# Reading a linear-attention memory in products of 136 columns, numerators beside denominators, three products to a PSUM bank

## The chip, the cores and the metric

The kernel runs on one core of one Trainium2 chip. Times are device microseconds (us) of that core. TensorE (PE in the profile, PEld for its weight loads) multiplies into PSUM; VectorE (DVE), ScalarE (ACT) and GpSimd (POOL) work elementwise; SyncE (SP) issues most transfers. The metric is the median over the runs shown.

## What is computed

The reference mixes two branches on the same input x (2048 rows of 512, bf16) with a gate from x: `g * a + (1 - g) * b`. Branch b is a gated feed-forward block with 1792 hidden columns. Branch a is attention with 32 heads of 16 columns over four segments of 512 rows. Inside a segment it is causal softmax attention; from segment to segment a memory is carried per head. Cut to what matters for the change:

```
pq = phi(qs)                                  # phi(t) = t+1 where t>0, else exp(t)
num = einsum('bhld,bhde->bhle', pq, M)
den = einsum('bhld,bhd->bhl', pq, z)[..., None] + 1e-06
o = g * (num / den) + (1.0 - g) * a_dot       # g = sigmoid(beta), one per head
M = M + einsum('bhld,bhle->bhde', phi(ks), vs);  z = z + sum over l of phi(ks)
```

The first segment has no memory to read; the three others do.

## The kernel before, in words

**Tiling.** The 32 heads form four chunks of eight heads, 128 rows of head columns each (`NC8` = 4). Queries and keys lie transposed, 128 head columns by 512 positions (QT, ktb, pq for phi of the queries). A segment's 512 positions are four tiles of 128 (`KT` = 4). The memory M of a chunk is spread over a 128 x 128 block-diagonal matrix Mn (eight blocks of 16 x 16, made by a mask in `u_mask`, L571), z over a 128 x 8 matrix Mz (L582).

**The memory read.** In `u_den` (L595), once per pair of chunks, eight products of 8 columns (L603) put the denominators of two chunks into a PSUM tile zd; VectorE adds 1e-6 (L610), and a period later takes the reciprocal (L613) and multiplies by gh = sigmoid(beta) (L614), into rdm. In `mem_num` (L628), once per chunk, four products of 128 columns (L632) fill a PSUM tile mn, and one VectorE instruction (L636) multiplies it with rdm into tm. A DMA on SP's queue (L644) transposes tm into mT, and `add_mem` (L698) adds mT to the chunk's softmax part in oT some periods later.

**What sets the order.** The order of all instructions is written out by a planner in the kernel's Python. Its main loop (L992) runs over 72 "visits", here called periods. Each begins with a group of query-key products into the only lg tile (`group_qk`, L647), whose exponential on ScalarE (L658) gives pT, and GpSimd clears the parts above the diagonal (L662). Eight periods or so make a chunk; two periods after its last one a "lump" (L934) runs the 64 small products with V into two PSUM tiles od (`pv`, L667), which VectorE then transposes to oq, normalises (L690, L691), transposes back into oT (L696) and, from the second segment on, adds mT to (L699).

Between these the planner fills TensorE's time with units of other streams: keys kT (L375), queries qT (L289), values vT (L413) and zT (L429), the feed-forward's gate gT (L472), up uT (L493) and down dT (L509) products, and the output projection aT (L532). A unit has TensorE time, VectorE time and a due period; `fill_to` (L781) takes the one with the smallest due period, corrected by how much VectorE work is booked (`backlog`). Each unit's result is evicted from PSUM by VectorE (L312, L499, L314, L538) or, where the planner sees room, by ScalarE (`cast`, L305). Deferred work stands in `due` and is run at its period (`later`, L319).

All these PSUM tiles (kT, qT, vT, zT, gT, uT, dT, aT, od, zd, mn, MT) share one pool of four banks (L82, `pgen`); lg has the other four. A unit's first product waits until the bank that it was given has been evicted. VectorE, ScalarE and TensorE each work in their order.

Before the change, the numerator of a chunk is asked for one period ahead of the chunk's last (L1037) and runs in the middle of the next period's filling (L1031), with 0.3 us of TensorE and `EVAC` = 0.69 us of VectorE booked for it (L968); `can_num` (L974) forces the denominators where they are late.

A second path for large inputs, `general()` (L1104), is built behind a test of the inputs' size and doesn't run with these inputs.

Of the kernel before, what the change touches and what calls it, by code (L numbers as in the profile page):

```python
# [13 lines left out]
P = 128  # L14
D = 512
H = 32
# [37 lines left out]
def kernel(  # L54
# [29 lines left out]
    def const(shape, dtype, name):  # L84
        return cpool.tile(shape, dtype, name=name, tag=name)
# [10 lines left out]
    bm = const([P, 8, 17], BF, "bm")  # L96
    eo = const([P, 2], F32, "eo")
    beta = const([P, H], BF, "beta")
    gh = const([P, H], F32, "gh")
    og = const([P, H], F32, "og")  # L100
    Macc = const([P, NC8, 2, 17], F32, "Macc")
    Mn = [const([P, NC8, 128], BF, f"Mn{i}") for i in range(2)]
    Mz = [const([P, NC8, 8], BF, f"Mz{i}") for i in range(2)]
    rdm = [const([P, KT, H], F32, f"rdm{i}") for i in range(2)]
    ktb = const([P, NC8, L], BF, "ktb")
    pk = const([P, KT, D], BF, "pk")
    G = [const([P, HS, L], BF, f"G{i}") for i in range(NG)]
# [17 lines left out]
    def gen(name):  # L125
        return pgen.tile([P, 512], F32, name=name, tag="gen")
# [85 lines left out]
        nc.gpsimd.memset(Macc[:, :, :, :], 0.0)  # L212

    def setup_beta():
        eb = wk2.tile([P, H], F32, name="eb", tag="eb")
        nc.scalar.activation(eb[:, :], beta[:, :], AF.Exp, scale=-1.0)
        nc.vector.tensor_scalar_add(eb[:, :], eb[:, :], 1.0)
        nc.vector.reciprocal(gh[:, :], eb[:, :])
        nc.vector.tensor_scalar(out=og[:, :], in0=gh[:, :], scalar1=-1.0, scalar2=1.0,
                                op0=ALU.mult, op1=ALU.add)  # L220
        for j in range(4):
            r = slice(32 * j, 32 * j + 32)
            nc.vector.tensor_copy(
                ogs[r, :, :],
                og[r, :].rearrange("p (c j q) -> p c j q", c=NC8, j=4)[:, :, j, :])
# [93 lines left out]
    def later(n, f):  # L319
        due.setdefault(clock[0] + n, []).append(f)  # L320
# [5 lines left out]
    def count(key):  # L326
        return done.get(key, 0)
# [243 lines left out]
    def u_mask(s):  # L571
        def half(h0):
            for c in (h0, h0 + 1):
                nc.vector.tensor_tensor(
                    out=Mn[s % 2][:, c, :].rearrange("q (j p d) -> q j p d", j=4, p=2),
                    in0=Macc[:, c, None, :, 0:16].to_broadcast((P, 4, 2, DH)),
                    in1=bm[:, :, 0:16].rearrange("q (j p) d -> q j p d", j=4), op=ALU.mult)
            passed(0.0, 0.6)
            done["Mn", s] = count(("Mn", s)) + 1

        def f():
            nc.vector.tensor_tensor(  # L582
                out=Mz[s % 2][:, :, :].rearrange("q c (j p) -> q c j p", j=4),
                in0=Macc[:, :, None, :, 16].to_broadcast((P, NC8, 4, 2)),
                in1=bm[:, None, :, 16].to_broadcast((P, NC8, 8))
                .rearrange("q c (j p) -> q c j p", j=4), op=ALU.mult)
# [8 lines left out]
    def u_den(s, pair):  # L595
        def f():
            assert general_now[0] or ("q", s, 2 * pair) in ready
            T = gen("zd")
            Tv = T[:, 0:KT * 16].rearrange("p (q h) -> p q h", q=KT)
            for cc in range(2):  # L600
                c = 2 * pair + cc
                for qq in range(KT):
                    nc.tensor.matmul(Tv[:, qq, 8 * cc:8 * cc + 8],  # L603
                                     lhsT=pq[:, c, qq * P:(qq + 1) * P],
                                     rhs=Mz[s % 2][:, c, :], start=True, stop=True)
                if cc == 0:
                    yield 0.12
            h0 = 16 * pair
            r = rdm[s % 2][:, :, h0:h0 + 16]
            nc.vector.tensor_scalar_add(r, Tv, 1e-6)  # L610

            def f_inv():
                nc.vector.reciprocal(r, r)  # L613
                nc.vector.tensor_tensor(out=r, in0=r,  # L614
                                        in1=gh[:, None, h0:h0 + 16].to_broadcast((P, KT, 16)),
                                        op=ALU.mult)
                passed(0.0, 0.8)
                done["inv", s] = count(("inv", s)) + 1
            if general_now[0]:
                f_inv()  # L620
            else:
                later(1, f_inv)
            return 0.12
        return 0.24, 0.22, f

    tms = {}

    def mem_num(s, c):  # L628
        assert general_now[0] or (count(("Mn", s)) > c // 2 and count(("inv", s)) > c // 2)
        T = gen("mn")  # L630
        for qq in range(KT):
            nc.tensor.matmul(T[:, qq * P:(qq + 1) * P],  # L632
                             lhsT=pq[:, c, qq * P:(qq + 1) * P], rhs=Mn[s % 2][:, c, :],
                             start=True, stop=True)
        tm = wk2.tile([P, KT, 8, DH], BF, name="tm", tag="tm")
        nc.vector.tensor_tensor(  # L636
            out=tm[:, :, :, :], in0=T[:, :].rearrange("p (q h d) -> p q h d", q=KT, h=8),
            in1=rdm[s % 2][:, :, 8 * c:8 * c + 8, None].to_broadcast((P, KT, 8, DH)), op=ALU.mult)
        mT = wk2.tile([P, L], BF, name="mT", tag="mT")
        mTv = mT[:, :].rearrange("p (q t) -> p q t", q=KT)  # L640
        if general_now[0]:
            turn(mTv, tm[:, :, :, :].rearrange("p q h d -> p q (h d)"))
        else:
            nc.sync.dma_start_transpose(mTv, tm[:, :, :, :].rearrange("p q h d -> p (q h d)"))  # L644
        tms[(s, c)] = mT

    def group_qk(pieces):  # L647
        lg = plg.tile([P, 4, 512], F32, name="lg", tag="lg")
# [78 lines left out]
    def passed(pe, dve=0.0):  # L727
        backlog[0] = max(0.0, backlog[0] - pe) + dve
        t_pe[0] += pe
# [155 lines left out]
    us = []  # L885
    for s in range(NSEG - 1):
        us.append(unit(u_mask(s + 1), 0, None, lambda s=s: count(("M", s)) == 1))
        us += [unit(u_den(s + 1, pair), NP * s + 16 + 9 * pair, ("den", s + 1),
                    lambda s=s, pair=pair: ("q", s + 1, 2 * pair) in ready)
               for pair in range(2)]  # L890
    streams.append(Stream("M", us))

    us = [unit(u_absmax_x(2, (18, 20, 22, 25)), 17, None, lambda: clock[0] >= 17),
# [71 lines left out]
        if s > 0:  # L965
            later(4, f_add)

    def numerator(s, c):  # L968
        room_for_bank()
        mem_num(s, c)  # L970
        done["num", s] = count(("num", s)) + 1
        passed(0.3, EVAC)

    def can_num(s, c):  # L974
        if count(("den", s)) <= c // 2 and ("q", s, c - c % 2) in ready:
            need(("den", s), c // 2 + 1)
        return count(("Mn", s)) > c // 2 and count(("inv", s)) > c // 2

    asked = []
    pending = []  # L980
    visits = []
    for i in range(0, NSEG * NC8, 2):
# [9 lines left out]
    for pieces in visits:  # L992
# [41 lines left out]
        fill_to(goal)  # L1034
        t_pe[0] = max(t_pe[0], ready_at)
        limit[0] = 0.0
        for i in range(NC8, NSEG * NC8):  # L1037
            if last(i) - 1 == clock[0]:
                asked.append((i // NC8, i % NC8))
        if asked and can_num(*asked[0]):  # L1040
            pending.append(lambda a=asked.pop(0): numerator(*a))
    limit[0] = 1e9
    fill_to(t_pe[0] + TAIL_FILL * 0.42)
    assert not asked
    for f in pending:
        f()
    for _, i in lumps:
# [56 lines left out]
    def general():  # L1104
# [4 lines left out]
        for s in range(NSEG):  # L1109
# [16 lines left out]
            if s > 0:  # L1126
                for c in range(0, NC8, 2):
                    phi_now(pq[:, c:c + 2, :], QT[:, c:c + 2, :])
                run(u_mask(s))
                run(u_den(s, 0))  # L1130
                run(u_den(s, 1))
            neg = G[(s + 1) % NG][:, 8, 0:P]
            nc.gpsimd.memset(neg, 0.0)
            nc.gpsimd.affine_select(out=neg, in_=neg, pattern=[[-1, P]], compare_op=ALU.is_ge,
                                    fill=-1e9 * DH ** 0.5, base=0, channel_multiplier=1)
            for c in range(NC8):
                o2 = wk2.tile([P, 16, 2, DH], BF, name="o2", tag="o2")
                if s > 0:
                    mem_num(s, c)
                tiles = {}  # L1140
                for b in range(5):
                    t = ptp.tile([P, 4, 512], BF, name="pT", tag="pT")
                    tiles[b] = (t, 0)
                    if 1 <= b <= 3:
                        tiles[NB - b] = (t, L - 64 * b)
                general_blocks(s, c, tiles)
                oq = pv(s, c, tiles)
                for p in range(2):
                    norm(c, p, oq[p], o2)
                back(c, o2, oT)  # L1150
                if s > 0:
                    add_mem(s, c, oT)
# [54 lines left out]
```

## Time and profile before

| | us |
|---|---|
| median of 3 runs (268.22 to 268.45) | 268.25 |
| the profiled execution | 268.14 |
| its span, first to last instruction | 266.3 |
| VectorE's busy time in 28 to 250 us (222 us) | 171.2 |
| TensorE's busy time in 28 to 250 us | 221.95 |
| granted TensorE clock | 1.0 |

The groups of the memory read, with number, busy time and mean of one:

| line | engine | what | number | busy us | mean ns |
|---|---|---|---|---|---|
| L603 | PE | zd, 128 x 8 | 48 | 2.1 | 166 |
| L632 | PE | mn, 128 x 128 | 48 | 4.6 | 219 |
| L610 | DVE | sum with 1e-6, 128 x 64 from PSUM | 6 | 1.3 | 216 |
| L613 | DVE | reciprocal, 128 x 64 | 6 | 3.2 | 526 |
| L614 | DVE | times gh, 128 x 64 | 6 | 1.8 | 308 |
| L636 | DVE | tm, 128 x 512 from PSUM | 12 | 8.2 | 682 |
| L644 | SP | DMA transpose of tm | 12 | | 2.4 us to landing |

A product's row lasts until its result has drained, so products overlap: what one costs TensorE is the distance from its start to the next start. Likewise two VectorE instructions that don't depend on each other overlap a little at their ends.

### The profile page before, as it was taken

The numbers are of one execution on the slowest core, as the hardware profiler recorded it, in microseconds if no ns is written. First come the engines' busy times: TensorE is split into PE (matmuls) and PEld (weight loads), VectorE is DVE, ScalarE is ACT, GpSimd is POOL, SyncE is SP. The second block draws the span as 40 slices with busy tenths as digits, with TensorE's granted clock in tenths as the row PEclk, the third lists the DMA queues.
The fourth block names the chain that finished last, engine by engine and source line by source line (L and its number), as shares of the span: only waits on it lengthen the run. The fifth ranks groups of instructions, "written<-read, shape, count | busy, mean of one in ns | idle before, by whom it ended". The sixth has DMA issues, their size and how long they took to land.

```text
span 266.3 us, 6883 instructions
## 1 busy us (share of the span) xinstructions
PE 261.7 (98%) x2865; PEld 117.4 (44%) x2865; DVE 200.7 (75%) x394; ACT 209.7 (79%) x164; POOL 155.0 (58%) x298
## 2 busy tenths in 40 slices
PE   7999999999999999999999999999999999999995
PEld 4454434344443444444445344444444444444443
DVE  2999574969569887698887858695978759698364
ACT  4236889988998899889999999889989987657511
POOL 3000158896716979678940899687694099654500
PEclk9999999999999999999999999999999999999999
DMA  7999931200322001300023010301000110002202
GB/s 217 328 194 290 323 78 39 42 4 1 68 57 42 2 0 42 79 6 20 2 59 86 0 23 20 64 20 22 20 23 23 46 22 8 14 20 42 41 22 84
DMA packets 30410, 16.60 MB, mean 62 GB/s; under 512 B 20008, under 2 KB 29096, under 8 KB 30376
## 3 DMA queue, kind: packets, MB, share of 16 engines
q1 hardware_dynamic: 30232, 16.07, 24.2%
q8 instruction: 23, 0.38, 0.6%
q14 instruction: 11, 0.09, 0.1%
q10 hardware_dynamic: 144, 0.07, 0.1%
HBM read 8.14 MB, written 2.10 MB: 38 GB/s over the span
## 4 chain that ended last, share of the span: by engine, by line
PE 98%; DVE 1%; issue 0%; DVEq 0%
PE uT L493 19%; PE dT L509 19%; PE gT L472 19%; PE lg L653 9%; PE od L678 7%; PE kT L375 5%; PE qT L289 5%; PE aT L532 5%; PE vT L413 5%; PE mn L632 1%; PE warm L166 1%; PE zT L429 1%; PE MT L560 1%; DVE tB L538 1%; PE x0T L183 1%; PE zd L603 0%
## 5 line engine op out<-in xcount | busy, mean ns | idle before, releaser
L662 POOL TENSOR_SCALAR_AFFINE_SELECT pT<-pT 64x256 bf16<-64x256 bf16 x256 | 112.2, 438 | 94.6 <-ACT pT L658 81.8
L658 ACT ACTIVATE pT<-lg 128x2048 bf16<-128x2048 f32 x72 | 135.1, 1876 | 22.5 <-PE lg L653 21.2
L493 PE MATMUL uT<-x,wup 128*128 128x512 bf16 x224 | 60.6, 380 | 0.0
L472 PE MATMUL gT<-x,wga 128*128 128x512 bf16 x224 | 55.6, 379 | 0.0
L509 PE MATMUL dT<-wdn,G 128*128 128x512 bf16 x224 | 53.9, 380 | 0.0
L499 DVE TENSOR_TENSOR G<-uT,G 128x512 bf16<-128x512 f32 x56 | 38.1, 683 | 6.2 <-PE uT L493 5.7
L385 POOL TENSOR_SCALAR KTm<-ktb,eo 128x512 bf16<-128x512 bf16 x26 | 40.6, 1575 | 1.3
L685 DVE STREAM_TRANSPOSE oq<-od 128x512 f32<-128x512 f32 x32 | 21.0, 696 | 19.9 <-PE od L678 19.9
L472 PEld LDWEIGHTS <-wga 128*128 128x128 bf16 x224 | 20.7, 98 | 24.5 <-issue 2.4
L509 PEld LDWEIGHTS <-G 128*128 128x128 bf16 x224 | 20.5, 98 | 24.3 <-issue 2.8
L493 PEld LDWEIGHTS <-wup 128*128 128x128 bf16 x224 | 20.2, 98 | 24.5 <-issue 4.7
L653 PE MATMUL lg<-QT,KTm 32*128 32x192 bf16 (+7 forms) x512 | 28.6, 287 | 0.0
L312 DVE CAST G<-gT 128x512 bf16<-128x512 f32 x25 | 17.2, 686 | 5.8 <-PE gT L472 5.6
L653 PEld LDWEIGHTS <-KTm 32*128 32x128 bf16 x512 | 8.5, 92 | 29.5 <-issue 29.5
L678 PE MATMUL od<-pT,V 64*32 64x128 bf16 (+7 forms) x512 | 19.3, 284 | 0.0
L678 PE MATMUL od<-pT,Vs 64*32 64x128 bf16 (+7 forms) x512 | 18.9, 284 | 0.0
L487 ACT ACTIVATE G<-G 128x3584 bf16<-128x3584 bf16 x6 | 18.8, 3182 | 0.0
L691 DVE SCALAR_TENSOR_TENSOR o<-oq,ogs,rden 128x256 bf16<-128x256 f32 x32 | 17.3, 541 | 1.1
L375 PE MATMUL kT<-x,wk 128*128 128x512 bf16 x64 | 16.6, 379 | 0.4 <-DVE eo L204 0.4
L289 PE MATMUL qT<-x,wq 128*128 128x512 bf16 x64 | 16.6, 379 | 0.0
L538 DVE SCALAR_TENSOR_TENSOR tB<-aT,gct,tB 128x512 bf16<-128x512 f32 (+1 forms) x18 | 12.0, 685 | 5.7 <-PE aT L532 5.5
L532 PE MATMUL aT<-wo,oT 128*128 128x512 bf16 (+1 forms) x72 | 16.2, 356 | 0.0
(95 smaller groups left out, 269.7 us busy)
## 6 DMA issues: line engine op xcount, KB each, us to landing
wup<-in_B_w_up_dram SPq DMA_DIRECT2D x1, 1792.0 KB, 9.7
wdn<-in_B_w_down_dram SPq DMA_DIRECT2D x1, 1792.0 KB
out_dram<-tB SPq DMA_DIRECT2D x13, 128.0 KB, 1.7
wga<-in_B_w_gate_dram SPq DMA_DIRECT2D x1, 1280.0 KB, 10.4
Vs<-V SPq DMA_DIRECT2D x8, 144.0 KB, 3.1
G<-in_A_x_dram SPq DMA_DIRECT2D x2, 256.0 KB, 2.8
wk<-in_A_wk_dram SPq DMA_DIRECT2D x2, 256.0 KB, 4.5
wq<-in_A_wq_dram SPq DMA_DIRECT2D x1, 512.0 KB, 5.6
```

What stands on the lines that cost most here:

```text
L289: nc.tensor.matmul(T[:, :], lhsT=wq[:, fc, c * P:(c + 1) * P], rhs=xS[s % NX][:, fc, :], start=(fc == 0), stop=(fc == FC - 1))
L375: nc.tensor.matmul(T[:, :], lhsT=wk[:, fc, c * P:(c + 1) * P], rhs=xS[s % NX][:, fc, :], start=(fc == 0), stop=(fc == FC - 1))
L385: eng.tensor_scalar(out=KTm[:, (NC8 * s + c) % NK, :, p, :], in0=ktb[:, c, :].rearrange("q (b k) -> q b k", b=NB), scalar1=eo[:, p:p + 1], ...
L472: nc.tensor.matmul(T[:, :], lhsT=wga[:, fc, hs * P:(hs + 1) * P], rhs=xS[s % NX][:, fc, :], start=(fc == 0), stop=(fc == FC - 1))
L493: nc.tensor.matmul(T[:, :], lhsT=wup[:, fc, hs * P:(hs + 1) * P], rhs=xS[s % NX][:, fc, :], start=(fc == 0), stop=(fc == FC - 1))
L499: nc.vector.tensor_tensor(out=g, in0=T[:, :], in1=g, op=ALU.mult)
L509: nc.tensor.matmul(T[:, :], lhsT=G[s % NG][:, hs, qt * P:(qt + 1) * P], rhs=wdn[:, hs, :], start=(hs == 0), stop=(hs == HS - 1))
L532: nc.tensor.matmul(T[:, 0:w], lhsT=oT[:, fc, qt * P:(qt + 1) * P], rhs=wo[:, fc, d0:d0 + w], start=(fc == 0), stop=(fc == FC - 1))
L653: nc.tensor.matmul(lg[:, j, off:off + n], lhsT=KTm[rows, i % NK, b].rearrange("r p k -> r (p k)"), rhs=QT[rows, i % NC8, 64 * b:L], start= ...
L658: nc.scalar.activation(pT[:, :, :], lg[:, :, :], AF.Exp, scale=DH ** -0.5)
L662: nc.gpsimd.affine_select(out=v, in_=v, pattern=[[0, 4], [1, 64]], compare_op=ALU.is_ge, fill=0.0, base=0, channel_multiplier=-1)
L678: nc.tensor.matmul(od[p][32 * j:32 * j + 32, 64 * b:L], lhsT=w[:, 18 * h:18 * h + 32], rhs=t[rows, j, off:off + n], start=(b == 0), stop=( ...
```

## The change

Mz and rdm go; Mn becomes 136 columns wide, 128 numerator columns and 8 denominator columns, so one product gives both for one tile of positions. `u_den` and `mem_num` are replaced by `mem_read`. The 16 products of a segment (four chunks by four tiles) are read three to a bank, in six reads (products 0-2, 3-5, 6-8, 9-11, 12-14 and 15); where a read holds products of two chunks, its VectorE work is done in two parts, except the reciprocal. The denominators are multiplied by eb = 1 + exp(-beta) in the same instruction that adds 1e-6, so that the reciprocal is already the factor for the numerator. The planner books 0.18 us of TensorE and 1.1 us of VectorE for a read and asks for the six reads at periods counted from the chunks' last ones.

```diff
-    Mn = [const([P, NC8, 128], BF, f"Mn{i}") for i in range(2)]
-    Mz = [const([P, NC8, 8], BF, f"Mz{i}") for i in range(2)]
-    rdm = [const([P, KT, H], F32, f"rdm{i}") for i in range(2)]
+    Mn = [const([P, NC8, 136], BF, f"Mn{i}") for i in range(2)]
...
+    def mem_read(s, m):
+        T = gen("mn")
+        todo = [divmod(t, KT) for t in range(3 * m, min(3 * m + 3, NC8 * KT))]
+        rd = wk2.tile([P, 3, 8], F32, name="rd", tag="rd")
+        parts = []
+        for i, (c, qq) in enumerate(todo):
...
+            nc.tensor.matmul(T[:, 136 * i:136 * i + 136], lhsT=pq[:, c, qq * P:(qq + 1) * P],
+                             rhs=Mn[s % 2][:, c, :], start=True, stop=True)
+            if parts and parts[-1][0] == c:
+                parts[-1][3] += 1
+            else:
+                parts.append([c, qq, i, 1])
+        Tv = T[:, 0:408].rearrange("p (k e) -> p k e", k=3)
+        for c, qq, i, n in parts:
+            nc.vector.scalar_tensor_tensor(
+                out=rd[:, i:i + n, :], in0=Tv[:, i:i + n, 128:136], scalar=1e-6,
+                in1=eb[:, None, 8 * c:8 * c + 8].to_broadcast((P, n, 8)),
+                op0=ALU.add, op1=ALU.mult)
+        nc.vector.reciprocal(rd[:, 0:len(todo), :], rd[:, 0:len(todo), :])
+        for c, qq, i, n in parts:
+            if qq == 0:
+                halves[s, c] = wk2.tile([P, KT, 8, DH], BF, name="tm", tag="tm")
+            tm = halves[s, c]
+            nc.vector.tensor_tensor(
+                out=tm[:, qq:qq + n, :, :],
+                in0=Tv[:, i:i + n, 0:128].rearrange("p q (h d) -> p q h d", h=8),
+                in1=rd[:, i:i + n, :, None].to_broadcast((P, n, 8, DH)), op=ALU.mult)
+            if qq + n < KT:
+                continue
...
+                nc.sync.dma_start_transpose(mTv, tm[:, :, :, :].rearrange("p q h d -> p (q h d)"))
+            tms[(s, c)] = mT
+            done["num", s] = count(("num", s)) + 1
...
-        us += [unit(u_den(s + 1, pair), NP * s + 16 + 9 * pair, ("den", s + 1),
-                    lambda s=s, pair=pair: ("q", s + 1, 2 * pair) in ready)
-               for pair in range(2)]
...
-    def numerator(s, c):
+    def read(s, m):
         room_for_bank()
-        mem_num(s, c)
-        done["num", s] = count(("num", s)) + 1
-        passed(0.3, EVAC)
+        mem_read(s, m)
+        passed(0.18, 1.1)
...
+    reads = [(last(NC8 * s + c) - back_, s, m) for s in range(1, NSEG)
+             for c, back_, m in ((0, 2, 0), (0, 1, 1), (1, 1, 2), (2, 1, 3), (3, 2, 4), (3, 1, 5))]
...
-        for i in range(NC8, NSEG * NC8):
-            if last(i) - 1 == clock[0]:
-                asked.append((i // NC8, i % NC8))
-        if asked and can_num(*asked[0]):
-            pending.append(lambda a=asked.pop(0): numerator(*a))
+        if reads and reads[0][0] <= clock[0] and can_read(*reads[0][1:]):
+            pending.append(lambda a=reads.pop(0)[1:]: read(*a))
```

More of the change, by code (lines that the diff above doesn't have):

```diff
@@ L98 @@
     beta = const([P, H], BF, "beta")
-    gh = const([P, H], F32, "gh")
+    eb = const([P, H], F32, "eb")
     og = const([P, H], F32, "og")
     Macc = const([P, NC8, 2, 17], F32, "Macc")
-    Mn = [const([P, NC8, 128], BF, f"Mn{i}") for i in range(2)]
-    Mz = [const([P, NC8, 8], BF, f"Mz{i}") for i in range(2)]
-    rdm = [const([P, KT, H], F32, f"rdm{i}") for i in range(2)]
+    Mn = [const([P, NC8, 136], BF, f"Mn{i}") for i in range(2)]
     ktb = const([P, NC8, L], BF, "ktb")
@@ L214, in setup_beta @@
     def setup_beta():
-        eb = wk2.tile([P, H], F32, name="eb", tag="eb")
+        gh = wk2.tile([P, H], F32, name="gh", tag="gh")
         nc.scalar.activation(eb[:, :], beta[:, :], AF.Exp, scale=-1.0)
@@ L574, in half @@
                 nc.vector.tensor_tensor(
-                    out=Mn[s % 2][:, c, :].rearrange("q (j p d) -> q j p d", j=4, p=2),
+                    out=Mn[s % 2][:, c, 0:128].rearrange("q (j p d) -> q j p d", j=4, p=2),
                     in0=Macc[:, c, None, :, 0:16].to_broadcast((P, 4, 2, DH)),
@@ L582, in f @@
             nc.vector.tensor_tensor(
-                out=Mz[s % 2][:, :, :].rearrange("q c (j p) -> q c j p", j=4),
+                out=Mn[s % 2][:, :, 128:136].rearrange("q c (j p) -> q c j p", j=4),
                 in0=Macc[:, :, None, :, 16].to_broadcast((P, NC8, 4, 2)),
@@ L593, in u_mask @@
         return 0.0, 0.2, f
[L595 to L618, printed above, removed]
+    tms = {}
@@ new lines @@
+    halves = {}
+    def mem_read(s, m):
[4 more added lines that the diff above has]
+        for i, (c, qq) in enumerate(todo):
+            assert general_now[0] or (count(("Mn", s)) > c // 2 and ("q", s, c - c % 2) in ready)
+            nc.tensor.matmul(T[:, 136 * i:136 * i + 136], lhsT=pq[:, c, qq * P:(qq + 1) * P],
[21 more added lines that the diff above has]
+                continue
+            mT = wk2.tile([P, L], BF, name="mT", tag="mT")
+            mTv = mT[:, :].rearrange("p (q t) -> p q t", q=KT)
@@ L619, in f @@
             if general_now[0]:
-                f_inv()
+                turn(mTv, tm[:, :, :, :].rearrange("p q h d -> p q (h d)"))
             else:
[L622 to L645, printed above, removed]
@@ L966, in lump, with can_read @@
             later(4, f_add)
-    def numerator(s, c):
+    def read(s, m):
         room_for_bank()
-        mem_num(s, c)
-        done["num", s] = count(("num", s)) + 1
-        passed(0.3, EVAC)
[L974 to L979, printed above, removed]
+        mem_read(s, m)
+        passed(0.18, 1.1)
+    def can_read(s, m):
+        cs = {t // KT for t in range(3 * m, min(3 * m + 3, NC8 * KT))}
+        return all(count(("Mn", s)) > c // 2 and ("q", s, c - c % 2) in ready for c in cs)
+    reads = [(last(NC8 * s + c) - back_, s, m) for s in range(1, NSEG)
+             for c, back_, m in ((0, 2, 0), (0, 1, 1), (1, 1, 2), (2, 1, 3), (3, 2, 4), (3, 1, 5))]
     pending = []
@@ L1036 @@
         limit[0] = 0.0
-        for i in range(NC8, NSEG * NC8):
-            if last(i) - 1 == clock[0]:
-                asked.append((i // NC8, i % NC8))
-        if asked and can_num(*asked[0]):
-            pending.append(lambda a=asked.pop(0): numerator(*a))
+        if reads and reads[0][0] <= clock[0] and can_read(*reads[0][1:]):
+            pending.append(lambda a=reads.pop(0)[1:]: read(*a))
     limit[0] = 1e9
     fill_to(t_pe[0] + TAIL_FILL * 0.42)
-    assert not asked
+    assert not reads
     for f in pending:
@@ L1129, in general @@
                 run(u_mask(s))
-                run(u_den(s, 0))
-                run(u_den(s, 1))
             neg = G[(s + 1) % NG][:, 8, 0:P]
@@ L1137, in general @@
                 o2 = wk2.tile([P, 16, 2, DH], BF, name="o2", tag="o2")
-                if s > 0:
-                    mem_num(s, c)
+                for m in ((0, 1), (2,), (3,), (4, 5))[c] if s > 0 else ():
+                    mem_read(s, m)
                 tiles = {}
```

## The prediction

> **What bounds the kernel now.** I read the busy table first, then the chain that ended last, then the groups by line with shapes kept apart, then the instructions in order of time around the memory read.
>
> ```profile
> span 266.3 us, 6883 instructions
> PE 261.7 (98%) x2865; PEld 117.4 (44%) x2865; DVE 200.7 (75%) x394; ACT 209.7 (79%) x164; POOL 155.0 (58%) x298
> PE 98%; DVE 1%; issue 0%; DVEq 0%
> ```
>
> TensorE is the path: its products stand one behind the other from start to end, and the chain runs along it for 98% of the span. So a product that goes saves its own share of TensorE's time, and nothing else is worth anything unless it makes TensorE wait. The second question is whether it ever waits now. In order of time (start, length, instruction) two places show what the removed and the widened products cost, and a third shows a wait:
>
> ```profile
> 73.29 0.34 PE L603 MATMUL zd<-Mz,pq 128*128 128x8 bf16 x8
> 97.53 0.39 PE L632 MATMUL mn<-Mn,pq 128*128 128x128 bf16 x4
> ...
> 136.31 0.40 PE L653 MATMUL lg<-QT,KTm 32*128 32x448 bf16 x8
> 136.64 0.39 PE L678 MATMUL od<-pT,V 64*32 64x512 bf16 x1
> 137.06 0.39 PE L678 MATMUL od<-pT,Vs 64*32 64x512 bf16 x1
> ```
>
> The two od products of 136.64 and 137.06 belong to the two banks of one chunk and elsewhere start 3 ns apart; here the second waits 0.42 us for its bank. VectorE, in the same stretch, is why:
>
> ```profile
> 133.30 0.68 DVE L636 TENSOR_TENSOR tm<-mn,rdm 128x512 bf16<-128x512 f32 x1
> 133.89 0.69 DVE L574 TENSOR_TENSOR Mn<-Macc,bm 128x128 bf16<-128x128 f32 x2
> 134.51 0.70 DVE L696 STREAM_TRANSPOSE oT<-o 128x512 bf16<-128x512 bf16 x1
> 135.13 0.55 DVE L346 TENSOR_SCALAR ktb<-ktb 128x1024 bf16<-128x1024 bf16 x1
> 135.72 0.69 DVE L351 TENSOR_TENSOR ktb<-phe,ktb 128x1024 bf16<-128x1024 bf16 x1
> 136.32 0.68 DVE L499 TENSOR_TENSOR G<-uT,G 128x512 bf16<-128x512 f32 x1
> ```
>
> VectorE runs from 127.41 (the oq transposes of the chunk before) to 137.00 without a gap, 9.59 us; the product uT at its end frees the bank at 137.00. So the cover is thin: VectorE is idle a quarter of the span, but not here. A like wait of 0.25 us stands at 227.0, where GpSimd's selects are late. I found no other.
>
> **Part 1, TensorE.** Eight products of 8 columns take 0.34 us with 166 ns for one alone: (340 - 166)/7 = 25 ns from start to start. 48 go: -1.2 us. Four of 128 columns: (390 - 219)/3 = 57 ns; those of 256 columns (the last aT) stand 109 ns apart, so 136 columns cost 8/128 of 53 = 3.3 ns more: 48 x 3.3 = +0.16 us. In the changed order the weights are loaded 48 times fewer; loads already lie beside products. Changes between full-array and split-array products, at about 95 ns each, are 166 in both orders. Sum: **-1.04 us**. Bounds: nothing gained at the widest (136 columns at the 109 ns of 256 would be +2.5, which the even steps between the rows exclude), -1.2 if the 8 columns are free.
>
> **Part 2, VectorE's work.** In a crowded stretch an instruction starts before the last has ended: the 512-column evictions stand 0.60 apart (133.30 to 133.89) with 0.68 each, 0.08 less than the row; one that needs its predecessor's result starts 0.035 after it. Removed per pair of chunks: sum 0.13 (0.215 less 0.08), reciprocal 0.56, product 0.14, so 6 x 0.83 = 5.0 us; and 12 tm of 0.60, 7.2 us. Added, 18 reads. None of the new shapes is in the trace, so by neighbours: the add-and-scale from the bank between 0.15 (4 columns from a bank, L442) and 0.28 (128 columns, L437), I take 0.21, that of L610; the reciprocal of 24 between 0.24 (16) and 0.35 (32), I take 0.29; tm of 384, 256, 128 columns between 0.28 (L437) and 0.68, on the line between them 0.55, 0.41, 0.28. A read of one part: 0.245 + 0.33 + 0.47 = 1.04 us; of two parts 1.24; the last (one product) 0.68. Per segment 3 x 1.04 + 2 x 1.24 + 0.68 = 6.3, in all 18.9. Net **+6.7 us of VectorE** (from 4 to 9 by the ends), with one cast more on it. Beside TensorE's work, this is nothing where VectorE has slack; the planner books 1.1 for a read, so it does not overlook it. Masks, beta's setup (gh and eb change places) and the 12 transposing DMAs keep their number; those land in 2.4 us and are needed some four periods later, and SP's queue passes them over one or two output writes. The general path does not run.
>
> **Part 3, where the slack is missing.** A read now holds its bank through three to five VectorE instructions. The first waits for the last product of the three; behind it on VectorE stand the evictions of gT, uT and aT, and for their banks waits TensorE. The changed kernel was built, not run, so its order is known. I summed rows per period (a period is one trip of the loop at L992 and begins with its lg products; 72 in all) along that order, VectorE against TensorE, and followed the bank of each tile where VectorE is behind.
>
> Periods 34 to 38 (the stretch above). The changed order has in VectorE's run the reads of products 12 to 14 and of product 15, instead of one tm, and od's second bank is freed by the eviction of aT, which stands behind the two ktb instructions. So the run is 9.59 - 0.60 + 1.04 + 0.68 + 0.66 = 11.4 us from the oq transposes, which start 1.28 after the first od. TensorE's work from that od to the next: 34 products at 0.216, four of 0.06, four lg at 0.425, od 1.2: 10.5 us. Wait 1.28 + 11.4 + 0.06 - 10.5 = 2.2 us, against 0.42 now: **+1.8** (1.2 to 2.3 by the ends of part 2).
>
> Periods 39 to 41. Reads 0 and 1 of the next segment stand in neighbouring periods with the gates. From period 39's start the eviction of its uT ends at 0.33 (lg) + 8 x 0.216 + 0.2 to arrive + 0.6 = 2.87; then 0.68 (norm), 0.75 (gates, 83.08 to 83.83), gT 0.60, read 1.04, uT 0.60, oT 0.63, pq 0.55, gT 0.60: 8.3. The down product that takes this last bank is due at 7.6 (periods 39 and 40 with 10 and 9 products, 2.6 and 2.55, and 2.45 of period 41): **+0.75** (0 to 1.1). Before, nothing waits here.
>
> At 227.0 seven dT products now stand ahead of od: its wait of 0.25 goes, **-0.25** (-0.25 to 0). Elsewhere the same sums leave 0.1 to 0.5 us to spare.
>
> Sum: -1.04 + 1.8 + 0.75 - 0.25 = +1.3. The profiled execution took 268.14 (span 266.3), 0.1 under the median of 268.25. 268.14 + 1.3 = **269.4 us**, its own range 268.8 to 270.2.
>
> [...] VectorE runs 394 instructions now and 431 in the changed order. Its dependent instructions show a gap of 35 ns, its independent ones none. [...]
>
> **Rivals.**
> - The reads stay covered, and TensorE's saving is all: 268.1 - 1.0 - 0.25 + some tenths = 267.2. For it: in 222 us VectorE is idle for 50, and four banks let it lag (around 80 to 88 it runs 8 us in one piece and no product waits). It holds if the two reads of periods 35 and 36 together stay under 0.9 us and the later one falls behind an idle moment. Against: the bounds above put them at no less than 1.2. Chance 0.17.
> - One of the two places waits, the other not: 268.3 (267.7 to 268.8). Chance 0.17.
> - VectorE becomes the pace more widely, one mechanism: TensorE takes the next bank before a read has left it. All 6.7 exposed would give 274; a third of it beyond my two places gives 271.5. Against: 98% of TensorE and the spare tenths. It decides from 0.2 us more per read. Chance 0.12 for over 270.2.
> - That the change does not do what it says is excluded by the order: no product of 8 columns is left, 48 of 136 stand there.
>
> **The numbers.** Forecast 0.54, covered 0.17, one place 0.17, wider 0.12. About 0.2% is what a measurement of this kernel can tell from no change: 267.7 to 268.8. Faster 0.18, within 0.17, slower 0.65. The range leaves out most of the covered case and the far end of the wide one: 267.5 to 271.0.
>
> **What would show it.** Right: no zd, read products 59 ns apart, VectorE at about 207 us (78%); in the period list a second od product over a microsecond behind the first near 138, and a gap before a dT near 148. Wrong: those products 3 ns apart and the span shorter by about 1.0 (then the reads are shorter than their neighbours or VectorE's run starts earlier); or a new wait of GpSimd or ScalarE, which I hold at nothing since their instructions keep their number to within three casts.

## The result, and the profile after

| | before | after |
|---|---|---|
| median, us | 268.22 (22 runs, 268.05 to 270.14) | 269.39 (22 runs, 268.48 to 271.84) |
| ratio to before | | 1.004, 95% interval 1.0025 to 1.0055 |
| the profiled execution | 268.14 | 269.79 |
| its span | 266.3 | 267.9 |
| first lg product to last product | 234.83 | 235.92 |

The change makes the kernel 0.4% slower. The last row leaves out the first 28 us, in which executions differ whatever the kernel (last section). In that stretch the profiled executions differ by 1.09 us. One execution of a kernel further below (e8) ran in a slower state of the chip, at 299.63 us and a granted clock of 0.85, and is left out of its figures.

The lines of the page after that answer to those shown of before:

```profile
span 267.9 us, 6815 instructions
PE 261.5 (98%) x2817; PEld 116.2 (43%) x2817; DVE 204.1 (76%) x431; ACT 208.9 (78%) x163; POOL 156.4 (58%) x298
PE 91%; DVE 6%; issue 1%; DVEq 0%
```

TensorE has 48 products less and is as busy as before (261.5 us against 261.7): a product's row reaches past the next one's start (for 512 columns rows of 380 ns, starts 216 ns apart), so the busy time hardly shows what a product costs. The third line tells more: the chain that ended last ran along TensorE for 98% and now for 91%; 6% has gone to VectorE, so TensorE now waits for VectorE on its way. The waits themselves are far shorter than 6% of the span, as the next lists show.

The new groups, with shapes kept apart:

```profile
L604 PE MATMUL mn<-Mn,pq 128*128 128x136 bf16 x48 | 5.8, 223 | 0.0
L612 DVE SCALAR_TENSOR_TENSOR rd<-mn,eb 128x24 f32<-128x24 f32 x9 | 1.5, 169 | 1.1 <-PE mn L604 1.1
L616 DVE RECIPROCAL rd<-rd 128x24 f32<-128x24 f32 x15 | 4.5, 303 | 0.5
L621 DVE TENSOR_TENSOR tm<-mn,rd 128x384 bf16<-128x384 f32 x9 | 5.0, 557 | 0.3
```

The 18 reads have 19.2 us of VectorE rows; what they replace had 14.5 (1.3 + 3.2 + 1.8 + 8.2). And the waits, in order of time, around the end of the first segment that reads a memory:

```profile
133.32 0.23 PE L604 MATMUL mn<-Mn,pq 128*128 128x136 bf16 x1
133.90 1.02 PE L287 MATMUL qT<-x,wq 128*128 128x512 bf16 x4 [0.36 <-DVE G L497]
135.19 0.38 PE L530 MATMUL aT<-wo,oT 128*128 128x512 bf16 x1 [0.26 <-DVE G L310]
...
138.41 0.39 PE L667 MATMUL od<-pT,V 64*32 64x512 bf16 x1
139.14 0.39 PE L667 MATMUL od<-pT,Vs 64*32 64x512 bf16 x1 [0.34 <-DVE tB L536]
```

Brackets show idle time ahead of a row, after the end of the row before; what a wait costs is its start-to-start distance less the usual one. That gives 0.53 before qT (0.587 less 0.059), 0.42 before aT (0.636 less 0.216) and 0.72 at od (0.724 against 0.003). VectorE's order of time in that stretch names the late work:

```profile
135.65 0.16 DVE L612 SCALAR_TENSOR_TENSOR rd<-mn,eb 128x8 f32<-128x8 f32 x1
135.84 0.20 DVE L616 RECIPROCAL rd<-rd 128x8 f32<-128x8 f32 x1
136.07 0.29 DVE L621 TENSOR_TENSOR tm<-mn,rd 128x128 bf16<-128x128 f32 x1
136.28 0.48 DVE L572 TENSOR_TENSOR Mn<-Macc,bm 128x128 bf16<-128x128 f32 x2
...
137.73 0.69 DVE L349 TENSOR_TENSOR ktb<-phe,ktb 128x1024 bf16<-128x1024 bf16 x1
138.34 0.74 DVE L536 SCALAR_TENSOR_TENSOR tB<-aT,gct,tB 128x512 bf16<-128x512 f32 x1
```

The eviction of aT into tB, which frees od's second bank, ends at 139.08, behind the last read, Mn, oT and two ktb instructions. A wait of 0.44 stands before a dT (0.651 less 0.216):

```profile
156.53 0.81 PE L470 MATMUL gT<-x,wga 128*128 128x512 bf16 x3
157.61 0.59 PE L507 MATMUL dT<-wdn,G 128*128 128x512 bf16 x2 [0.27 <-DVE G L310]
```

One stop had no place in the prediction. The 64 products of MT (the sums for the new memory, L558), which before ran in one piece of 0.67 us, break off after the 60th, for 0.70 us, and the profile names no releaser:

```profile
174.58 0.63 PE L558 MATMUL MT<-V,pk 128*32 128x34 bf16 x60
175.74 0.20 PE L558 MATMUL MT<-V,pk 128*32 128x34 bf16 x4 [0.53 <-issue]
```

I call it the hole. The od of 244.3 waits 0.12 in all (1.226 against 1.106 us for its 64 products), and the wait of 0.25 at 227.0 is gone.

### The profile page after: what moved, and what is told of

It reads as the page before. It is cut to its first block, busy times and chain, and to the rows that moved or that the text cites. A ratio compares the mean times of both kernels' runs of the same rounds, so it can differ in the third digit from the quotient of the medians.

```text
span 267.9 us, 6815 instructions
## 1 busy us (share of the span) xinstructions
PE 261.5 (98%) x2817; PEld 116.2 (43%) x2817; DVE 204.1 (76%) x431; ACT 208.9 (78%) x163; POOL 156.4 (58%) x298
## 4 chain that ended last, share of the span: by engine, by line
PE 91%; DVE 6%; issue 1%; DVEq 0%
PE dT L507 18%; PE uT L491 18%; PE gT L470 17%; PE lg L642 8%; PE od L667 7%; PE kT L373 5%; PE qT L287 5%; PE vT L411 5%; PE aT L530 5%; DVE G L497 1%; PE warm L164 1%; DVE G L310 1%; PE mn L604 1%; DVE tB L536 1%; PE MT L558 1%
## 5 line engine op out<-in xcount | busy, mean ns | idle before, releaser
L470 PE MATMUL gT<-x,wga 128*128 128x512 bf16 x224 | 57.0, 380 | 0.0
L507 PE MATMUL dT<-wdn,G 128*128 128x512 bf16 x224 | 53.1, 380 | 0.3 <-DVE G L310 0.3
L383 POOL TENSOR_SCALAR KTm<-ktb,eo 128x512 bf16<-128x512 bf16 x26 | 41.4, 1603 | 1.3
L310 DVE CAST G<-gT 128x512 bf16<-128x512 f32 x28 | 19.2, 685 | 5.7 <-PE gT L470 5.1
L530 PE MATMUL aT<-wo,oT 128*128 128x512 bf16 (+1 forms) x72 | 17.2, 357 | 0.3 <-DVE G L310 0.3
L667 PEld LDWEIGHTS <-V 64*32 64x32 bf16 x512 | 13.1, 92 | 6.0 <-issue 2.8
```

The lines of the kernel that those rows point to most:

```text
L383: eng.tensor_scalar(out=KTm[:, (NC8 * s + c) % NK, :, p, :], in0=ktb[:, c, :].rearrange("q (b k) -> q b k", b=NB), scalar1=eo[:, p:p + 1], ...
L470: nc.tensor.matmul(T[:, :], lhsT=wga[:, fc, hs * P:(hs + 1) * P], rhs=xS[s % NX][:, fc, :], start=(fc == 0), stop=(fc == FC - 1))
L507: nc.tensor.matmul(T[:, :], lhsT=G[s % NG][:, hs, qt * P:(qt + 1) * P], rhs=wdn[:, hs, :], start=(hs == 0), stop=(hs == HS - 1))
L530: nc.tensor.matmul(T[:, 0:w], lhsT=oT[:, fc, qt * P:(qt + 1) * P], rhs=wo[:, fc, d0:d0 + w], start=(fc == 0), stop=(fc == FC - 1))
L667: nc.tensor.matmul(od[p][32 * j:32 * j + 32, 64 * b:L], lhsT=w[:, 18 * h:18 * h + 32], rhs=t[rows, j, off:off + n], start=(b == 0), stop=( ...
```

## The experiments

**The theory** from the two traces: TensorE's saving is real, and three things eat it: VectorE late in two places (its extra work, and where the reads stand), and the hole, which is TensorE waiting for its own instructions. **The rivals**: the reads' VectorE work is the price everywhere; the order of the reads alone is the price; the hole belongs to the changed order.

One table carries them all. The ratios are to runs of before on the same chip, whose medians were 268.17 (beside e1 to e4), 268.46 (e5 to e8) and 268.19 (e9 to e12); they are estimated from all these runs, and so are not quite the quotients of the medians. "Stretch" is from the first lg product to the start of the last product in the profiled execution. "Place 1" sums the waits from mn to od near 133 to 139, "place 2" is the one ahead of dT (or the unit in its stead) near 157, "others" are the waits at other od groups, units and lg groups (the table leaves out what is under 0.06; the 0.08 of e12 under "hole" stands at 115 us and is told of below).

| kernel | median | ratio, 95% interval | stretch | place 1 | place 2 | hole | others | stretch less waits |
|---|---|---|---|---|---|---|---|---|
| before | 268.22 | | 234.83 | 0.42 | 0 | 0 | 0.40 | 234.01 |
| after | 269.39 | 1.004, 1.0025 to 1.0055 | 235.92 | 1.67 | 0.44 | 0.70 | 0.12 | 232.99 |
| e1_bare_all | 267.93 | 0.9994, 0.9982 to 1.0005 | 234.39 | 1.00 | 0 | 0.38 | 0 | 233.01 |
| e2_bare_p1 | 268.58 | 1.0017, 1.0008 to 1.0026 | 234.82 | 1.00 | 0.52 | 0.18 | 0.12 | 233.00 |
| e3_bare_p2 | 269.20 | 1.0039, 1.0026 to 1.0052 | 235.93 | 1.67 | 0 | 1.02 | 0.24 | 233.00 |
| e4_zd_twice | 269.65 | 1.0057, 1.0044 to 1.007 | 236.03 | 0.43 | 0 | 0 | 0.40 | 235.20 |
| e5_after_no_small_warm | 270.24 | 1.004, 1.0014 to 1.0066 | 235.26 | 1.67 | 0.44 | 0 | 0.13 | 233.02 |
| e6_before_no_small_warm | 268.42 | 1.002, 0.9997 to 1.0043 | 234.88 | 0.44 | 0 | 0 | 0.44 | 234.00 |
| e7_fold | 268.69 | 1.0011, 0.9999 to 1.0022 | 235.22 | 1.49 | 0.51 | 0.21 | 0 | 233.01 |
| e8_early | 269.40 | 1.0045, 1.0028 to 1.0061 | 236.10 | 0.23 | 0 | 0.59 | 2.21 | 233.07 |
| e9_after_more_warm | 268.75 | 1.0033, 1.0016 to 1.0051 | 235.23 | 1.67 | 0.44 | 0 | 0.12 | 233.00 |
| e12_before_more_warm | 268.32 | 1.0007, 0.9988 to 1.0026 | 234.91 | 0.42 | 0 | 0.08 | 0.40 | 234.01 |
| e11_early1_more_warm | 267.50 | 0.9985, 0.9965 to 1.0005 | 233.96 | 0.23 | 0 | 0 | 0.71 | 233.02 |
| e10_fold_early1_more_warm | 266.49 | 0.9941, 0.992 to 0.9961 | 233.06 | 0 | 0 | 0 | 0 | 233.06 |

The last column is the reading to learn from. For every kernel with products of 136 columns, whatever its waits, it comes out at 233.0 to 233.1; for before, e6 and e12, with their separate products of 8 and 128 columns, at 234.0. So no wait by which these kernels differ is left out, and TensorE's own saving is 1.01 us (234.01 less 233.00). A wait that all of them share would stay in the column unseen.

Of the "others" of before, 0.15 are two waits for ScalarE that hardly show as idle time, since the row of the product ahead lasts 380 ns: the lg groups of 109.30 and 122.77 start 51 and 52 ns after ScalarE's exponential has read the lg tile, 385 ns after the product ahead of them where 312 is usual. In order of time, before:

```profile
120.84 1.88 ACT L658 ACTIVATE pT<-lg 128x2048 bf16<-128x2048 f32 x1 [0.31 <-PE lg L653]
...
121.95 0.81 PE L493 MATMUL uT<-x,wup 128*128 128x512 bf16 x3
...
122.77 0.40 PE L653 MATMUL lg<-QT,KTm 32*128 32x512 bf16 x4
```

The exponential ends at 122.72; the last of the three uT products starts at 122.38. Before, e4, e6 and e12 have both waits; after and the kernels made from it have neither.

### Reads without their denominators

```diff
+        bare = not general_now[0]        # e2: and s == 1 and m >= 4; e3: and s == 2 and m == 0
+        if not bare:
             for c, qq, i, n in parts:
                 nc.vector.scalar_tensor_tensor(...)
             nc.vector.reciprocal(rd[:, 0:len(todo), :], rd[:, 0:len(todo), :])
...
-                in1=rd[:, i:i + n, :, None].to_broadcast((P, n, 8, DH)), op=ALU.mult)
+                in1=(eb[:, None, 8 * c:8 * c + 8, None] if bare else rd[:, i:i + n, :, None])
+                .to_broadcast((P, n, 8, DH)), op=ALU.mult)
```

> The changed kernel, its order of instructions kept, with the sum-and-scale and the reciprocal of every read left out (the numerators are multiplied by 1+exp(-beta) instead, so the memory part of the output is not the reference's). VectorE loses about 10 us of work, the products stay as they are. Theory (TensorE waits for banks behind the longer reads): the waits of periods 36 to 41 go, TensorE's saving of 1.0 is left, 267.2 to 267.6. Rival (the new order of the other units costs the time, not the reads' length): 269.4, waits where they were.

> As the run before, but the two instructions are left out in two reads alone, products 12 to 14 and 15 of segment 1 (the memory part of these is not the reference's). VectorE loses 0.53 + 0.42 = 0.95 us in its run of periods 34 to 38, where TensorE waited 1.67 us. Theory: 0.95 less, 268.4 to 268.6. Rival: 269.4.

> As the run before, but the two instructions are left out in one read alone, products 0 to 2 of segment 2 (the memory part of these is not the reference's). VectorE loses 0.53 us ahead of the eviction that the down product of 156.96 waited 0.44 us for. Theory: that wait goes, 0.4 us less, 269.0. Rival: 269.4.

e1 keeps the order of after, and VectorE has some 9 us of rows less. Its time came out 0.3 above the expected range: place 2 is gone, but place 1 keeps 1.00 of its 1.67, and the hole stays. e2 takes the two instructions away at the end of the first segment alone: place 1 goes to 1.00 as in e1, place 2 stays. e3 takes them away in one read of the next segment: place 2 goes, place 1 stays. So each place has its own cause in the reads that stand there, and what the other reads' denominators cost is at most the 0.12 under others. In place 1 the add, scale and reciprocal are worth 0.67; the other 0.6 over before remains with the reads bare. e3's time hardly moved, and can't tell the two expectations apart: its hole was 1.02 in the profiled execution. The hole has another size in each profiled execution.

### What a product of 8 columns costs

```diff
-                for qq in range(KT):
+                for qq in sorted(2 * list(range(KT))):
                     nc.tensor.matmul(Tv[:, qq, 8 * cc:8 * cc + 8],
```

> The kernel before with each of the 48 products of 8 columns done twice. Theory (25 ns from start to start on a TensorE that never rests): +1.2 us, 269.4. Rival (they lie free beside weight loads and waits): 268.2. [...]

In order of time, e4 (before with each of these products twice):

```profile
73.64 0.55 PE L603 MATMUL zd<-Mz,pq 128*128 128x8 bf16 x16
```

(0.55 - 0.166)/15 = 25.6 ns from start to start, and the stretch less waits grows by 1.19 us, 24.8 ns for each of 48. The 25 ns of the prediction hold. The median went up by 1.48 (interval of the ratio: 1.2 to 1.9 us).

### The hole, and where it stands in the instruction stream

The trace of after holds 23 transfers of 16 KB in a queue that the page calls "q8 instruction". 5634 products and weight loads by 23 are some 245 each; from one transfer's start to the next TensorE starts 254 of its instructions on average, if the last transfer, which starts after the last product, is left out. So TensorE's instructions come in blocks of about that number. Each hole comes after one of the transfers:

| kernel | transfer starts, us | takes | landed | TensorE goes on | after landing | hole |
|---|---|---|---|---|---|---|
| after | 172.80 | 1.35 | 174.15 | 175.74 | 1.6 | 0.70 |
| e1_bare_all | 171.88 | 0.88 | 172.76 | 174.36 | 1.6 | 0.38 |
| e2_bare_p1 | 172.47 | 0.98 | 173.45 | 174.90 | 1.45 | 0.18 |
| e3_bare_p2 | 172.37 | 1.40 | 173.77 | 175.17 | 1.4 | 1.02 |
| e7_fold | 172.17 | 1.10 | 173.27 | 174.73 | 1.45 | 0.21 |
| e8_early | 171.38 | 1.13 | 172.50 | 174.08 | 1.6 | 0.59 |

Whatever the transfer's start and length, TensorE goes on 1.4 to 1.6 us after it has landed. In that stretch the 64 od products end and the 64 MT products follow within 3 us, which fits a block that is used up before the next is there. In e7, which has one product less ahead of its MT group, the hole stands after the 61st product, not the 60th: in all six kernels 1885 products stand ahead of the hole. It keeps its place in the instruction stream, not in the work. To move the stream alone I changed the warming products at the very start:

```diff
-        for i in range(5):       # e9, e12 (e5, e6: unchanged)
+        for i in range(4):
...
-        for i in range(16):      # e5, e6: this loop left out
+        for i in range(48):      # with 64 columns each in place of 256
```

> After, with the 16 small products that only warm TensorE up at the very start left out (no output depends on them). Nothing later is moved; only every later product stands 16 products (32 of TensorE's instructions) earlier in its instruction stream, so that the refills of its instructions fall elsewhere. Theory (the hole of 0.2 to 1.0 us between the 60th and 61st product of the third MT group, seen in after and in the three bare kernels, is TensorE waiting for its next instructions, because the od and MT products behind that refill use them up in under 3 us): the hole is gone, the waits at mn, qT, od and dT stay as in after, 268.4 to 269.1. Rival (the hole belongs to the changed order, or to a bank or the memory sums): the hole stays at the same product, 269.2 to 269.6. Either way up to 0.5 us may go at the start itself, so the hole decides and not the time alone.

> Before, with the same 16 warming products left out. Its od and MT groups near 170 us then stand within 5 instructions of where after has them. Theory (instruction refill): a hole of 0.2 to 1.0 us comes into the last ten products of the third MT group, which had none in before; 267.9 to 269.0, with a start up to 0.5 us earlier against it. Rival (the hole belongs to the change): no hole, 267.7 to 268.2.

> After, with 48 small warming products of 64 columns in place of 16 of 256, and four large ones in place of five, so that about as long a start puts 31 products more (62 instructions) ahead of everything else. Theory (instruction refill): some 24 slow products now stand between the refill's boundary and the od products near 172 us, the block of 256 instructions lasts over 4 us instead of 2.9, and the hole in the third MT group is gone, as it was without the small products; the waits at mn, qT, od and dT stay; 268.5 to 269.0, and from the first query-key product to the end 0.2 to 1.0 us less than in after. Rival (dropping the small products took the hole away in some other way than by the count of instructions): the hole is back, 269.2 to 269.6.

> Before, with the same 48 small and four large warming products: the control for the start. Both theories: no hole in either, 268.0 to 268.5; what it differs from before by is the price of the other start, to be taken off the kernels beside it.

The third MT group of e9, in order of time:

```profile
173.97 0.40 PE L642 MATMUL lg<-QT,KTm 32*128 32x384 bf16 x8
174.30 0.67 PE L558 MATMUL MT<-V,pk 128*32 128x34 bf16 x64
```

The hole is gone with 31 products more ahead, as it was in e5 with 16 less, and the waits at places 1 and 2 are the same to 0.01 us. Median against its control e12: 268.75 - 268.32 = +0.43, where after and before lie 1.17 apart. That fits a hole worth some 0.7 us in the medians too, but the interval of each of the two ratios is 0.8 to 1.0 us wide, so the medians alone don't show it.

e6 failed to do what I expected: before, with its od and MT groups where after has them in the stream, showed no hole in its profiled execution. There the transfer started at 170.36, took 1.05 and landed at 171.41; the block ended at 172.97, 1.55 us later, within the 1.4 to 1.6 us of the table. The block lasted 3.03 us in e6, and 2.85 in after without its hole. That fits the theory, but it is a near miss, not the hole that I had asked for: that the same edit makes one in before isn't shown.

e12, the control, shows a small one where I had expected none. Its stream has before's order, 31 products later:

```profile
114.14 0.93 PE L413 MATMUL vT<-wv,x 128*128 128x448 bf16 x4
115.00 0.20 PEld L653 LDWEIGHTS <-KTm 32*128 32x128 bf16 x8 [0.37 <-issue]
115.09 0.40 PE L653 MATMUL lg<-QT,KTm 32*128 32x384 bf16 x8
```

From the last vT product to the lg product are 366 ns, where 282 are usual, 0.08 us more; ScalarE had read the lg tile 0.99 us before. A transfer landed at 113.72, 1.28 us ahead of the weight load. 2496 of TensorE's instructions stand ahead of that load in the trace, 3777 or 3778 ahead of the first instruction behind the hole in the six kernels: 1281 or 1282 apart. In after the transfer ahead of the hole (172.80) is the fifth behind the one of 114.50, which is the nearest to e12's stop; so five blocks make 1281 or 1282 instructions, some 256 each. So this stop too stands at the end of a block, and in before's order. At 0.08 us in one execution it is a small sign, but it speaks against the rival that the hole belongs to the changed order.

The profiled execution of e5 (270.39, by its median of 270.24) lost its time at the start (last section): its stretch is 0.66 shorter than that of after.

### Cheaper reads, and reads elsewhere

e7 folds 1 + exp(-beta) into the mask of the denominator columns, so that a read is two VectorE instructions:

```diff
-                in1=bm[:, None, :, 16].to_broadcast((P, NC8, 8))
-                .rearrange("q c (j p) -> q c j p", j=4), op=ALU.mult)
+                in1=bz[:, :, :].rearrange("q c (j p) -> q c j p", j=4), op=ALU.mult)  # bm's column x eb
...
+        nc.vector.reciprocal(rd[:, 0:n, :], Tv[:, :, 128:136])
+        nc.vector.tensor_tensor(out=tm[:, 3 * m:3 * m + n, :, :],
+            in0=Tv[:, :, 0:128].rearrange("p q (h d) -> p q h d", h=8),
+            in1=rd[:, 0:n, :, None].to_broadcast((P, n, 8, DH)), op=ALU.mult)
...
-        passed(0.18, 1.1)
+        passed(0.18, 0.85)
```

> After, with 1+exp(-beta) folded into the mask that makes the denominator columns, so that a read is one reciprocal from PSUM and one multiplication into one tm for all 16 products of the segment; 0.85 us booked instead of 1.1. It leaves out the sum of 1e-6 in the denominators. Reads then take about 0.86 us of VectorE (reciprocal 0.30, tm 0.56), 14.3 us in all against 19.1 in after. Theory (VectorE's lateness in two crowded places is the price): mn to qT, od at 138 and gT to dT lose half or more of what they have over the bare reads; the hole in the MT products stays; 268.2 to 268.9. Rival (the order and the six bank turns are the price, not VectorE's work): 269.2 to 269.5, the waits as in after.

e8 moves the last two reads of a segment; e11 and e10 move them in the first of these segments alone, and e10 has the fold as well:

```diff
-             for c, back_, m in (..., (2, 1, 3), (3, 2, 4), (3, 1, 5))]
+             for c, back_, m in (..., (2, 1, 3), (3, 4, 4), (3, 3, 5))]    # e8
+             for c, back_, m in (..., (2, 1, 3), (3, 4 if s == 1 else 2, 4), (3, 3 if s == 1 else 1, 5))]    # e11, e10
```

> After, with the last two reads of each segment asked for two periods earlier (four and three before the chunk's last instead of two and one), away from the new Mn, the oT and the ktb of the segment's end. Theory (price of a crowded place): the wait of 0.5 between mn and qT near 133 and most of the od wait at 138 go, VectorE has a hole before 139, 268.4 to 269.0. Rival (VectorE has nothing to spare anywhere near, the lateness only moves): waits of the same sum two periods earlier, 269.2 to 269.6.

> After with the other start, and with the last two reads two periods earlier in the first segment with a memory alone. Theory (place 1 is a matter of where two reads stand): mn to qT and qT to aT near 134 go, od at 138 keeps some 0.2, the rest stays as in after (gT to dT 0.4); 267.6 to 268.3, below the control. Rival (the lateness moves on): waits of over 0.5 come in later periods, 268.5 or more.

> The same with 1+exp(-beta) folded into the mask of the denominator columns, one reciprocal from PSUM and one multiplication a read (the sum of 1e-6 is left out). Theory (less VectorE work counts only where it is late): 0 to 0.3 us below the kernel with the reads earlier alone, 267.4 to 268.1. Rival (order alone): the same as it within 0.1.

e7 has 4.9 us of read rows less than after (14.2) and its time fell into the expected range, but not for the expected reason: place 1 lost 0.18 where half or more was expected, place 2 nothing; 0.5 us came from a smaller hole. In e8 place 1 fell from 1.67 to 0.23 and the lateness moved on, as the rival had it. Its dearest new wait, in order of time:

```profile
243.17 0.39 PE L667 MATMUL od<-pT,V 64*32 64x512 bf16 x1
244.28 0.37 PE L667 MATMUL od<-pT,Vs 64*32 64x512 bf16 x1 [0.72 <-DVE tm L621]
```

Here od's second bank is one that a read had, and the read's own tm is what is late. e11 keeps the old places in the later segments: place 1 at 0.23, place 2 gone, 0.71 elsewhere. So each of its expectations was half right: the time fell 0.1 below the theory's range, but 0.59 of the 0.71 are new waits between 160 and 172, as the rival had it. e10 has none of these waits left; its page and, in order of time, its od group:

```profile
span 264.8 us, 6848 instructions
PE 259.6 (98%) x2848; PEld 116.1 (44%) x2848; DVE 202.6 (77%) x403; ACT 208.1 (79%) x162; POOL 155.8 (59%) x298
PE 96%; DMA 2%; DVE 1%; SPq 0%; issue 0%; DVEq 0%
```

```profile
136.98 0.40 PE L638 MATMUL lg<-QT,KTm 32*128 32x448 bf16 x8
137.31 0.39 PE L663 MATMUL od<-pT,V 64*32 64x512 bf16 x1
137.31 0.39 PE L663 MATMUL od<-pT,Vs 64*32 64x512 bf16 x1
```

The two banks' first products start together, where before had 0.42 between them. VectorE is as busy as before (202.6 against 200.7); only where its work stands differs. e10 beats both kernels: 266.49, ratio 0.9941 (0.992 to 0.9961), without the sum of 1e-6. I had expected the fold to be worth 0 to 0.3 there; it was 1.0 by the medians and 0.90 by the stretch, since in e11 0.94 us of waits were left to take. The same fold took only 0.2 from places 1, 2 and the others of after. Its booking of 0.85 also moved units about, and how much of the 0.9 is work and how much order, these runs don't tell.

## Why the prediction was right, point by point

The time came out as forecast, 269.39 against 269.4, but in part by luck: the two places were sized 0.86 us too dear, and the hole (0.70) and the wait at 244 (0.12) were missed, which nearly cancels. In the stretch the terms add up to -1.01 + 1.25 + 0.44 - 0.25 - 0.15 + 0.70 + 0.12 = +1.1 us, against +1.3 forecast.

- **Part 1, TensorE.** Forecast -1.04, measured -1.01 (last column of the table); the 25 ns of a product of 8 columns by e4. Read products are 0.34 us for three, (340 - 223)/2 = 59 ns apart, as forecast.
- **Part 2, VectorE's work.** The estimates from neighbours held: reciprocal of 24 columns 0.303 (0.29), tm 0.557, 0.420 and 0.288 (0.55, 0.41, 0.28); the add-and-scale was 0.15 to 0.17, not 0.21. A read of one part took 1.01 us from its start at 132.16 to the next instruction (1.04), the last one 0.63 (0.68). The 207 us of busy time were too many (204.1): I had summed how long VectorE is held, and the gaps inside a read (0.03 us each, from 135.81 to 135.84 and 136.04 to 136.07 in the list above) are not busy time.
- **Part 3, periods 34 to 38.** The mechanism was right (VectorE without a gap, here from 128.34 to 139.08, and a late tB eviction behind the ktb instructions), the size not: 1.67 less 0.42 is +1.25 in place of +1.8. VectorE's run was 10.74 us, not 11.4. And it was not one wait at od: TensorE had already waited 0.95 of it for two other banks, ahead of qT and aT, which I had not followed.
- **Part 3, periods 39 to 41.** +0.44 in place of +0.75, by the mechanism that e3 shows. It stands in period 41 as worked out, at 157.2; the "near 148" of the last part set the period's time wrongly.
- **"I found no other" wait** was wrong: the two for ScalarE at 109.30 and 122.77 stood in before, and after lost them, 0.15 us that the forecast hasn't.
- **227.0**: its 0.25 went as forecast. **"Elsewhere 0.1 to 0.5 us to spare"** failed by 0.12 at 244.3.
- **What failed as a step** is the last sentence, which names a new wait of GpSimd or ScalarE as all that was left to fear, and the sum, which has no term for late instructions. The edit takes 96 instructions from TensorE's stream and so shifts where its blocks of instructions end; one such end fell among the od and MT products, which take 17 and 9 ns each.
- **Rivals.** "VectorE the pace more widely" is refuted as the price everywhere: by e1 to e3, all but 0.12 us of what the add, scale and reciprocal cost is paid in 3 of 18 reads. "Covered" falls with e1: even bare reads leave 1.00 in place 1. "One place" falls since both waited.

## What to carry to other kernels

When a saved product sits on a full engine, take the profiled time apart into that engine's own work and a list of its waits, and see that the rest comes out the same for every variant; then each wait can be bought separately. Here the saving (1.01 us) was real from the first, and became a gain of 1.7 us only when two reads were moved out of a crowded stretch, all were made cheaper, and the instruction stream was shifted; of the 1.7, before's own waits (0.82 in the table), which e10 has lost, are nearly half. A median that agrees with a forecast doesn't show its terms right.

## What the runs showed of the hardware that I had not expected

**Instructions can be late.** From the first product of the block before the hole to the first after it, TensorE took 3.03 to 3.87 us in the six kernels of that table. The block's own work is 2.85 us in after without its hole; for the rest, 0.18 to 1.02 us in the six, TensorE stood still. 64 products of MT take 598 ns and 64 of od 1106 ns up to the next unit's first product (56.10 and 45.59 in after), 9 and 17 ns each where one of 512 columns takes 216, so a block made of them doesn't last.

**The start differs from one execution to the next.** In before the kT products at the start, in order of time, then in e5:

```profile
6.05 2.76 PE L375 MATMUL kT<-x,wk 128*128 128x512 bf16 x12 [0.39 <-DVE eo L204]
```

```profile
6.14 4.10 PE L364 MATMUL kT<-x,wk 128*128 128x512 bf16 x10 [0.63 <-DMA wk<-in_A_wk_dram]
```

Twelve take 2.76 us in the one and ten 4.10 in the other: in e5 they stand 427 ns apart until 9.5 us, in before 226 and then 216; in after the first three distances are 380, 426 and 304, and 216 from 7.16 us on. The first lg product came at 28.00 in before, 28.46 in after, 29.86 in e5 and 29.66 in e11, and e5's runs fall into two groups, 268.3 to 268.7 (4) and 270.1 to 270.4 (7). The profiled execution of e5 belongs to the upper group; that the late start makes that group fits, but the starts of the other runs aren't on record. The granted clock of the page reads 9 (90% or more) in every slice of before and after all the same, and e5's is 1.0 over its execution. The step from the one distance to the other came by 6.28 us in before, at 7.16 in after and as late as 9.5 in e5. What makes it late in one run and not in the next wasn't tried.
